# Moving the second pair's preparation, dropping idle matmuls and copies' engine in early attention, and moving stores to GpSimd with sums loaded ahead in a fused attention and two-MLP kernel

## The chip, the cores and the metric

One Trainium2 chip, one of its cores. The metric is device time in microseconds (us) of one execution; the kernel before was run three times, and its median counts. TensorE is PE in the profile (its weight loads are PEld), VectorE is DVE, ScalarE is ACT, GpSimd is POOL, SyncE is SP. SPq and POOLq are the queues on which SP and POOL issue transfers (DMAs).

## The reference

Attention over 4 batches, 8 heads, 576 positions and 64 columns a head, with a causal mask and a bias from running sums of `s`; its output, 2304 tokens of 512 columns, goes through two MLPs (512 to 2048 to 512) with different activations:

```python
scores = scale * np.matmul(q, k.transpose(0, 1, 3, 2))
cum = np.cumsum(np.maximum(s, 0.0), axis=-1)
bias = -(cum[:, :, :, None] - cum[:, :, None, :])
scores = np.where(causal, -1000000000.0, scores + np.minimum(bias, 0.0))
attn = np.exp(scores - np.max(scores, axis=-1, keepdims=True))
attn = attn / (np.sum(attn, axis=-1, keepdims=True) + 1e-09)
x = np.matmul(attn, v)                       # heads side by side: 2304 x 512
h = x @ w_in1;  x = (h / (1 + np.exp(-1.702 * h))) @ w_out1
h = x @ w_in2;  P = a[0] + a[1]*h + a[2]*h*h + a[3]*h*h*h
Q = 1 + abs(b[0]) * abs(h) + abs(b[1]) * h*h
return (P / (Q + 1e-6)) @ w_out2
```

## The kernel before, in words

**Numbers.** Every fp32 operand of a product is split into a high and a low part, and a product is three matmuls (high by high, and the two mixed ones). Weights are split on the chip: `convert` loads half a unit of weights (512 KB, tile `raw`, in attention `stgA`) on SP's queue (L493, L495), works on it with ACT (L497, L499, L505) and DVE (L500, L501, L502, L504, L506; in attention L504 and L506 are POOL's), and leaves high and low parts in `u` or, for units that have no room yet, in `park`. `park` then writes these two parts to scratch memory `wd` (L542), and `fetch` reads a whole unit back later (L546). `raw` has four buffers.

**Attention** is one loop over j, 80 units (4 batches, 4 pairs of heads, 5 blocks of rows in the order 0, 1, 4, 2, 3; five units make a pair, twenty a batch). For unit j TensorE makes the scores (L251), DVE adds the mask and finds the row minimum (L285), ACT takes the exponential (L292), POOL scales the rows (L304). Three units later (two from j = 20) the rows are transposed on TensorE (L344; L323 and L327 for block 4) and copied out of PSUM by ACT, or by DVE where `COPY_V` names the (batch, block) (L351, L348, L324, L328); another unit later come the products with the values (L370). The operands of a pair are made one pair ahead by `prep`, a generator in two steps: transposes of k and then of q (L218), high parts on ACT (L176), low parts on DVE (L179), and copies of parts to other partitions by transfers on SP's queue (`kh<-kh` and `k<-qs`, L225). It also loads the bias rows (`k<-rows`, L204) that `store_sums` wrote before (L115 on SP, L113 on POOL). `pair_load` loads k and q of a pair (L145) and, when its `values` is called, v (L152, L156).

Between the steps of a unit `fill` puts work of the first MLP's units 0 to 4 for the batch before (`mlp1_first`: stage1 L562, out1 L586), paid by a credit of `FILL` / 20 a unit. While there is none yet (`cold`, up to j = 22) it issues `warm` instead: matmuls on zeros whose result nobody reads (L75). In attention the order on TensorE is that of the code; elsewhere, and on the other engines, a scheduler sets it.

**Behind attention** `mlp1_rest` runs the first MLP's units 5 to 11, and then 12 to 15, over 8 blocks of 288 tokens. A step (blk, j) is stage1 of one unit, its activation (`act1`: ACT L573, DVE L574, ACT L576, DVE L579) and, two steps later, out1 into four PSUM banks `a`. With the last unit of a block, four sums of earlier passes are loaded (`xp`, L636, SP), DVE adds them (L637), and the result is stored (L638, SP). `tick` issues half a conversion a step: units 12 to 15 first, then units 7 to 15 of the second MLP by way of `park`. Then comes the second MLP (`mlp2`: L562, L727).

SP issues its transfers in one order; one that waits holds up those behind it.

Of the kernel before, what the change touches and what calls it, by code (L numbers as in the profile page):

```python
# [10 lines left out]
F32 = mybir.dt.float32  # L11
# [5 lines left out]
ALU = mybir.AluOpType  # L17
# [12 lines left out]
P = 128  # L30
NQ = 5
KD = DM // P
NF = DF // P
F1 = 5
HB = S // 2
# [9 lines left out]
FILL = 33.0  # L45
AHEAD, AHEAD_0 = 2, 3
COPY_V = ((0, 0), (0, 4))
# [8 lines left out]
class Fused:  # L56
# [340 lines left out]
    def attention(self, att, mlp):  # L397
# [7 lines left out]
        nprep = iter(())  # L405
        self.sums_load(att)
        ld = self.pair_load(att, 0, 0, True)
# [4 lines left out]
        ld = self.pair_load(att, 0, 1)  # L412
        start()
        ld["values"]()
        self.store_sums()
        done = 0
        for j in range(n + AHEAD + 1):
# [16 lines left out]
            q = FILL / 20  # L434
            if j < n:
                self.unit_scores(att, units[j], 0)
                if j:
                    next(nprep, None)
            self.fill(q / 3, 1)
# [8 lines left out]
            if j < n and idx == 4:  # L448
                for _ in nprep:
                    pass  # L450
                g = b * NP + p + 2
                if g < NB * NP:
                    ld = self.pair_load(att, *divmod(g, NP))
                    ld["values"]()
            if k >= 0:
                self.unit_values(att, units[k])
# [78 lines left out]
    def park(self, buf, layer, f, half):  # L535
        nc = self.nc
        key = layer, f
        if half == 0:
            self.parked[key] = self.dram.tile([P, 4, 512], F32, name=f"wd{layer}_{f}")
        self.convert(self.source(layer, f, half), buf[:, 0], buf[:, 1])  # L540
        for i in range(2):
            nc.sync.dma_start(self.parked[key][:, half + 2 * i], buf[:, i].bitcast(F32))  # L542
# [79 lines left out]
    def mlp1_rest(self, pool, fs, src, dst, after_unit, at_block, last):  # L622
        nc = self.nc
        nblk = 2 * NB
        pend = []

        def flush():
# [3 lines left out]
            if j == len(fs) - 1:  # L631
                for d in range(KD):
                    st = self.spool.tile([P, HB], F32, name="st", tag="st", bufs=2)
                    xp = self.spool.tile([P, HB], F32, name="xp", tag="xp", bufs=2)
                    sl = np.s_[d * P : (d + 1) * P, blk * HB : (blk + 1) * HB]
                    nc.sync.dma_start(xp, src[sl])  # L636
                    nc.vector.tensor_tensor(st, accs[d][:, :HB], xp, ALU.add)  # L637
                    nc.sync.dma_start(dst[sl], st)  # L638
# [3 lines left out]
        for blk in range(nblk):  # L642
# [6 lines left out]
            for j, f in enumerate(fs):  # L649
# [12 lines left out]
                pend.append((blk, j, f, g, accs))  # L662
                self.tick()
# [247 lines left out]
```

## Time and profile before

| what | value |
|---|---|
| median of 3 runs (lowest, highest) | 1064.91 us (1062.80, 1066.14) |
| the profiled execution: time, span | 1062.4 us, 1060.6 us |
| busy in it: PE, PEld | 1029.6 us (97%), 942.3 us (89%) |
| busy in it: DVE, ACT, POOL | 805.7 us (76%), 722.8 us (68%), 259.4 us (24%) |
| chain that ended last, by engine | PE 73%, DMA 12%, DVE 6%, ACT 5% |

Attention ends near 327 us, the first MLP near 666 us. A busy PE is not a PE at its peak: the ends of matmuls are modelled, so how many matmuls of one shape fit into a stretch says more than the busy share. The share of the span is an average over stages with different limits; what a change in one stage is worth is read from the rows of that stage.

### The profile page before, as it was taken

Reading aid. Unit: us, or ns where it says so; the run is one execution under the profiler, and the core shown is the slowest. Engines: PE = TensorE matmul, PEld = TensorE weight load, DVE = VectorE, ACT = ScalarE, POOL = GpSimd, SP = SyncE. Lnnn points to the kernel's source line nnn. Section 1 sums busy time; section 2 is a strip of 40 time slices with the busy share of each in tenths; the row PEclk is TensorE's granted clock in tenths of the full one; section 3 lists DMA queues with packets and bytes.
Section 4 is the critical chain, followed back from the end, with each engine's and each line's share of the span. In section 5 each row is a group of like instructions: output and inputs, shape, how many; then the busy total and the mean of one; then the engine's idle time right before and its main releaser. Section 6 shows DMA issues by size and latency. Waiting matters only on the chain.

```text
span 1060.6 us, 19849 instructions
## 1 busy us (share of the span) xinstructions
PE 1029.6 (97%) x7073; PEld 942.3 (89%) x7073; DVE 805.7 (76%) x1874; ACT 722.8 (68%) x1668; POOL 259.4 (24%) x321
## 2 busy tenths in 40 slices
PE   6998999999999999998999999999999999999997
PEld 4767998898999899988999999998999999999996
DVE  6787767766644998884379344898998988989886
ACT  6898868978855675563265224787777777777765
POOL 4455734543420000000000000222222222222222
PEclk8999999999999999999999999999999999999999
DMA  8456455543215648995146546100010010100000
GB/s 183 120 153 163 112 148 157 137 138 82 53 46 222 204 160 277 300 305 175 46 125 209 188 124 243 48 30 30 2 47 14 15 46 1 31 30 1 31 1 30
DMA packets 88203, 117.31 MB, mean 111 GB/s; under 512 B 25728, under 2 KB 71808, under 8 KB 86508
## 3 DMA queue, kind: packets, MB, share of 16 engines
q1 hardware_dynamic: 87688, 115.43, 36.3%
q8 instruction: 56, 0.92, 0.4%
q0 software_dynamic: 192, 0.31, 0.2%
q14 instruction: 43, 0.35, 0.1%
q10 hardware_dynamic: 224, 0.30, 0.1%
HBM read 75.08 MB, written 32.05 MB: 101 GB/s over the span
## 4 chain that ended last, share of the span: by engine, by line
PE 73%; DMA 12%; DVE 6%; ACT 5%; issue 2%; POOL 1%; SPq 0%; ACTq 0%; DVEq 0%; POOLq 0%
PE h L562 29%; PE a L727 18%; PE a L586 12%; DMA raw<-in_moe_w_out_dram 5%; PE s L251 5%; PE O L370 4%; PE tp L344 2%; DMA stgA<-in_moe_w_in_dram 2%; DMA raw<-in_moe_w_in_dram 2%; DMA xp<-x 1%; DVE cvx L504 1%; DMA wd<-park 1%; ACT cvx L499 1%; DVE gl L579 1%; DVE cvx L502 1%
## 5 line engine op out<-in xcount | busy, mean ns | idle before, releaser
L710 POOL TENSOR_TENSOR gl<-u,gh 128x384 fp32r<-128x384 f32 x96 | 105.5, 1099 | 625.9 <-DMA x<-st 339.3
L562 PE MATMUL h<-x,u 128*128 128x288 f32 x1536 | 234.5, 298 | 5.3 <-ACT st L600 1.6
L586 PE MATMUL a<-gh,u 128*128 128x288 f32 x1024 | 232.3, 299 | 4.1 <-DVE st L637 3.0
L562 PEld LDWEIGHTS h<-x,u 128*128 128x128 f32 x1536 | 212.8, 188 | 11.2 <-DVE g L574 3.1
L586 PEld LDWEIGHTS a<-gh,u 128*128 128x128 f32 x1024 | 172.4, 188 | 10.2 <-DVE st L637 2.8
L562 PE MATMUL h<-y,u 128*128 128x384 f32 x864 | 166.2, 336 | 0.0
L562 PEld LDWEIGHTS h<-y,u 128*128 128x128 f32 x864 | 153.0, 188 | 6.3
L586 PE MATMUL a<-gl,u 128*128 128x288 f32 x512 | 148.6, 296 | 1.2 <-DVE gl L579 1.2
L727 PE MATMUL a<-u,gh 128*128 128x512 f32 x432 | 114.9, 394 | 0.9 <-ACT gh L708 0.9
L304 POOL TENSOR_SCALAR bt<-bt,sm 128x128 f32<-128x128 f32 (+3 forms) x129 | 71.3, 563 | 113.8 <-DVE sm L301 59.7
L586 PEld LDWEIGHTS a<-gl,u 128*128 128x128 f32 x512 | 96.3, 188 | 2.6 <-DVE gl L579 1.8
L292 ACT ACTIVATE bt<-bt,mn 128x128 f32<-128x128 f32 (+3 forms) x129 | 74.8, 580 | 29.7 <-DVE mn L285 28.1
L727 PEld LDWEIGHTS a<-u,gh 128*128 128x128 f32 x432 | 80.0, 188 | 14.9 <-ACT gh L708 1.7
L285 DVE CUSTOM_DVE_ANT_0 bt<-s,mask 128x128 f32<-128x128 f32 (+3 forms) x129 | 62.3, 483 | 37.1 <-PE s L251 31.2
L573 ACT ACTIVATE g<-h 128x288 f32<-128x288 f32 x128 | 51.1, 405 | 56.8 <-PE h L562 51.9
L576 ACT ACTIVATE gh<-g 128x288 fp32r<-128x288 f32 x128 | 55.7, 442 | 48.0 <-DVE g L574 47.3
L708 ACT ACTIVATE gh<-u 128x384 fp32r<-128x384 f32 x96 | 50.6, 527 | 54.2 <-DVE u L706 53.2
L693 ACT ACTIVATE y<-h,cf 128x384 f32<-128x384 f32 x96 | 55.6, 579 | 38.6 <-PE h L562 38.6
L574 DVE SCALAR_TENSOR_TENSOR g<-g,h 128x288 f32<-128x288 f32 x128 | 56.9, 448 | 32.4 <-ACT g L573 32.1
L251 PE MATMUL s<-k 68*128 68x256 f32 (+2 forms) x192 | 72.5, 382 | 8.7 <-DVE qs L179 4.8
L698 DVE SCALAR_TENSOR_TENSOR y<-s,cf,y 128x384 f32<-128x384 f32 x96 | 59.4, 618 | 24.5 <-ACT s L695 23.5
L706 DVE SCALAR_TENSOR_TENSOR u<-y,u 128x384 f32<-128x384 f32 x96 | 72.7, 757 | 1.1
(115 smaller groups left out, 2014.5 us busy)
## 6 DMA issues: line engine op xcount, KB each, us to landing
raw<-in_moe_w_in_dram SPq DMA_DIRECT2D x24, 512.0 KB
raw<-in_moe_w_out_dram SPq DMA_DIRECT2D x24, 512.0 KB
x<-st SPq DMA_DIRECT2D x64, 144.0 KB
wd<-park SPq DMA_DIRECT2D x36, 256.0 KB
u<-wd SPq DMA_DIRECT2D x8, 1024.0 KB
x2p<-st SPq DMA_DIRECT2D x32, 144.0 KB
xp<-x2p SPq DMA_DIRECT2D x32, 144.0 KB
xp<-x SPq DMA_DIRECT2D x32, 144.0 KB
```

The lines of the kernel that those rows point to most:

```text
L251: nc.tensor.matmul(sc[: c1 - c0, :w], lhsT=q[:, c0:c1], rhs=k[:, j0 : j0 + w], start=m == 0, stop=m == 1,)
L285: nc.vector.tensor_tensor_reduce(bt[:, j0 : j0 + w], sc[:, :w], mask, 1.0, 3.0e38 if i == 0 else mn[:, 0:1], ALU.add, ALU.min, mn[:, i : i ...
L292: ex = nc.scalar.activation(bt[:, :n], bt[:, :n], AF.Exp, bias=mn[:, i : i + 1], scale=-1.0, accum_out=sm[:, col : col + 1],)
L304: nc.gpsimd.tensor_scalar(bt[:, :n], bt[:, :n], inv[:, i : i + 1], 1.0, ALU.mult, ALU.mult)
L562: nc.tensor.matmul(ps_tile, lhsT=u[:, wl, kk * P : (kk + 1) * P], rhs=x(xl, kk), start=(n == 0), stop=(n == 3 * KD - 1),)
L574: nc.vector.scalar_tensor_tensor(g[:, :w], g[:, :w], 1.0, h, ALU.add, ALU.mult)
L576: nc.scalar.activation(gh[:, :w], g[:, :w], AF.Copy)
L586: nc.tensor.matmul(acc, lhsT=u[:, wl, d * P : (d + 1) * P], rhs=g[gl], start=(first and i == 0), stop=(last and i == 2),)
L698: nc.vector.scalar_tensor_tensor(y, s, cf[:, 7:8], y, ALU.mult, ALU.add)
L706: last = nc.vector.scalar_tensor_tensor(p, y, 2.0, p, ALU.subtract, ALU.mult)
L710: nc.gpsimd.tensor_tensor(gl, p, gh.bitcast(F32), ALU.subtract)
L727: nc.tensor.matmul(accs[m], lhsT=g[gl][:, m * P : (m + 1) * P], rhs=u[:, wl, :], start=(f == 0 and i == 0), stop=(f == NF - 1 and i == 2),)
```

## The change

In attention: `prep` of the second pair starts in unit 0 instead of unit 1; the stores of the sums are issued ahead of the first two pairs' values, and the second pair's values in unit 2; from j = 4 a cold unit issues its matmul on zeros only where j is a multiple of 5 (15 fewer); the filler's credit is 30 instead of 33 up to j = 42; DVE instead of ACT copies blocks 0, 1 and 4 of the second batch. Behind attention: the stores of parked parts and of the sums are issued on POOL; the four sums of a block are loaded in its third step, and the addition writes into the loaded tile, so that one set of four tiles takes the place of two tiles `st` and two `xp`.

```diff
--- before.py
+++ after.py
@@ -42,9 +42,9 @@
 PACE = 0.5
 AHEAD_F = (5, 6, 7)
 AHEAD_J = (35, 39, 43, 47, 51, 55)
-FILL = 33.0
+FILL, FILL_1 = 33.0, 30.0
 AHEAD, AHEAD_0 = 2, 3
-COPY_V = ((0, 0), (0, 4))
+COPY_V = ((0, 0), (0, 4), (1, 0), (1, 1), (1, 4))
 W2_SLOTS = 7
 CONV_J = (9, 12, 15, 18, 20, 22, 24, 26, 28, 30)
 CONV = [(f, 0) for f in range(F1)] + [(f, 1) for f in range(F1)]
@@ -410,9 +410,8 @@
             pass
         start = ld["values"]
         ld = self.pair_load(att, 0, 1)
+        self.store_sums()
         start()
-        ld["values"]()
-        self.store_sums()
         done = 0
         for j in range(n + AHEAD + 1):
             i = max(j - (AHEAD_0 if j < 20 else AHEAD), -1)
@@ -431,12 +430,11 @@
             if i >= 0 and i < n and units[i][0] and i % 20 == 1:
                 self.filler = chain(self.filler, self.mlp1_first(mlp, units[i][0] - 1))
                 self.cold = False
-            q = FILL / 20
+            q = (FILL_1 if j < 43 else FILL) / 20
             if j < n:
                 self.unit_scores(att, units[j], 0)
-                if j:
-                    next(nprep, None)
-            self.fill(q / 3, 1)
+                next(nprep, None)
+            self.fill(q / 3, j < 4 or j % 5 == 0)
             if 0 <= i < n:
                 tr = self.unit_transpose(att, units[i])
                 next(tr, None)
@@ -452,6 +450,8 @@
                 if g < NB * NP:
                     ld = self.pair_load(att, *divmod(g, NP))
                     ld["values"]()
+            if j == 2:
+                ld["values"]()
             if k >= 0:
                 self.unit_values(att, units[k])
             self.fill(q / 3, j < 4)
@@ -538,8 +538,9 @@
         if half == 0:
             self.parked[key] = self.dram.tile([P, 4, 512], F32, name=f"wd{layer}_{f}")
         self.convert(self.source(layer, f, half), buf[:, 0], buf[:, 1])
+        eng = nc.gpsimd if self.wide else nc.sync
         for i in range(2):
-            nc.sync.dma_start(self.parked[key][:, half + 2 * i], buf[:, i].bitcast(F32))
+            eng.dma_start(self.parked[key][:, half + 2 * i], buf[:, i].bitcast(F32))
 
     def fetch(self, u, layer, f):
         self.units[layer, f] = u
@@ -623,6 +624,18 @@
         nc = self.nc
         nblk = 2 * NB
         pend = []
+        xps = {}
+
+        def area(blk, d):
+            return np.s_[d * P : (d + 1) * P, blk * HB : (blk + 1) * HB]
+
+
+        def sums(blk):
+            xps[blk] = []
+            for d in range(KD):
+                xp = self.spool.tile([P, HB], F32, name="xp", tag="xp", bufs=KD)
+                nc.sync.dma_start(xp, src[area(blk, d)])
+                xps[blk].append(xp)
 
         def flush():
             blk, j, f, g, accs = pend.pop(0)
@@ -630,12 +643,9 @@
                 self.out1(accs[d][:, :HB], self.units[1, f], d, g, j == 0, j == len(fs) - 1)
             if j == len(fs) - 1:
                 for d in range(KD):
-                    st = self.spool.tile([P, HB], F32, name="st", tag="st", bufs=2)
-                    xp = self.spool.tile([P, HB], F32, name="xp", tag="xp", bufs=2)
-                    sl = np.s_[d * P : (d + 1) * P, blk * HB : (blk + 1) * HB]
-                    nc.sync.dma_start(xp, src[sl])
-                    nc.vector.tensor_tensor(st, accs[d][:, :HB], xp, ALU.add)
-                    nc.sync.dma_start(dst[sl], st)
+                    xp = xps[blk][d]
+                    nc.vector.tensor_tensor(xp, accs[d][:, :HB], xp, ALU.add)
+                    nc.gpsimd.dma_start(dst[area(blk, d)], xp)
             if blk == nblk - 1:
                 after_unit(f)
 
@@ -660,6 +670,8 @@
                 if accs is None:
                     accs = [self.bank("a", f"a2_{blk}_{f}_{d}") for d in range(KD)]
                 pend.append((blk, j, f, g, accs))
+                if j == 2:
+                    sums(blk)
                 self.tick()
         while pend:
             flush()
```

SP's order at the start, in the program before. `kn`, `qn` and `vn` are k, q and v of a pair, numbered by pair; `kh_1` and `k_1` belong to the second pair:

```order
L115 DMA rows<-stgA 16x2x576 x4
L145 DMA kn_2_369<-in_k_dram 96x2x384
L145 DMA qn_2_371<-in_q_dram 96x2x384
L204 DMA k_1_244<-rows 4x2304
L493 DMA stgA<-in_moe_w_in_dram 128x4x256
L81 DMA cf<-in_moe_a_dram 128x4
L82 DMA cf<-in_moe_b_dram 128x2
L145 DMA kn_3_596<-in_k_dram 96x2x384
L145 DMA qn_3_598<-in_q_dram 96x2x384
L225 DMA kh_1_242<-kh_1_242 64x1152
L225 DMA k_1_244<-qs_1_243 64x1152
```

And after the change, the four stores `rows<-stgA` standing just ahead of these rows:

```order
L152 DMA vn_1_193<-in_v_dram 128x4x64
L156 DMA vn_1_193<-in_v_dram 64x2x64
L204 DMA k_1_219<-rows 4x2304
L145 DMA kn_2_368<-in_k_dram 96x2x384
L145 DMA qn_2_370<-in_q_dram 96x2x384
L145 DMA kn_3_591<-in_k_dram 96x2x384
L493 DMA stgA<-in_moe_w_in_dram 128x4x256
L225 DMA kh_1_217<-kh_1_217 64x1152
L145 DMA qn_3_593<-in_q_dram 96x2x384
L81 DMA cf<-in_moe_a_dram 128x4
L82 DMA cf<-in_moe_b_dram 128x2
L225 DMA k_1_219<-qs_1_218 64x1152
```

The loads of k and q of the third pair moved from ahead of the bias rows of the second pair to behind them, and `k_1<-qs_1` stands behind the same loads as before.

SP's order behind attention, where unit 9 of the second MLP is parked, before:

```order
L493 DMA raw<-in_moe_w_in_dram 128x4x256
L542 DMA wd_9_6428<-park 128x512
L495 DMA raw<-in_moe_w_out_dram 128x1024
L542 DMA wd_9_6428<-park 128x512
L638 DMA x_12_5460<-st 128x288
L636 DMA xp<-x2p 128x288
L638 DMA x_12_5460<-st 128x288
L636 DMA xp<-x2p 128x288
L542 DMA wd_9_6428<-park 128x512
L493 DMA raw<-in_moe_w_in_dram 128x4x256
```

And after, at the same conversions:

```order
L493 DMA raw<-in_moe_w_in_dram 128x4x256
L495 DMA raw<-in_moe_w_out_dram 128x1024
L493 DMA raw<-in_moe_w_in_dram 128x4x256
L495 DMA raw<-in_moe_w_out_dram 128x1024
L493 DMA raw<-in_moe_w_in_dram 128x4x256
L637 DMA xp<-x2p 128x288
L495 DMA raw<-in_moe_w_out_dram 128x1024
L637 DMA xp<-x2p 128x288 x3
L493 DMA raw<-in_moe_w_in_dram 128x4x256
L495 DMA raw<-in_moe_w_out_dram 128x1024
```

No store is left between the loads of raw weights, only loads of sums.

POOL's order behind its last scaling of rows in attention; before, the next instruction there was the second MLP's first L710, and these rows now stand in between:

```order
+L648 DMA x_12_5445<-xp 128x288 x4
+L543 DMA wd_7_6071<-park 128x512 x4
+L543 DMA wd_8_6234<-park 128x512 x3
+L648 DMA x_12_5445<-xp 128x288 x4
+L543 DMA wd_8_6234<-park 128x512
+L543 DMA wd_9_6409<-park 128x512 x4
+L543 DMA wd_10_6564<-park 128x512 x4
+L543 DMA wd_11_6739<-park 128x512 x4
+L648 DMA x_12_5445<-xp 128x288
+L543 DMA wd_12_6898<-park 128x512
```

The stores of sums (L648) and of parked parts (L543) moved to POOL in the order in which they become ready.

## Rows read from the trace of the kernel before

**Rows 1.** Stretches: microseconds, busy time and instructions by engine, granted clock, DMA share, GB/s.

```profile
400.00:500.00 100.00, 94.10 (x679) 90.46 (x679) 79.29 (x175) 55.38 (x120) 0.00 (x0) 1.00 0.85 273
500.00:600.00 100.00, 100.00 (x757) 100.00 (x757) 62.88 (x141) 42.85 (x93) 0.00 (x0) 1.00 0.39 124
```

**Rows 2.** Whom PE waited for, 400 to 500 us: total, times, longest.

```profile
PE a L586 <- DVE st L637: 3.0, 3, 1.4
PE h L562 <- DVE g L574: 1.5, 4, 0.5
```

**Rows 3.** Groups of ACT, 400 to 500 us: busy, mean ns, idle time before, releasers.

```profile
L497 ACT ACTIVATE raw<-raw 128x512 int32<-128x512 uint32 x23 | 15.7, 681 | 34.5 <-DMA raw<-in_moe_w_in_dram 17.2 <-DMA raw<-in_moe_w_out_dram 17.1
```

**Rows 4.** Whom SP's queue waited for, 400 to 500 us.

```profile
SPq L542 <- ACT gh L576: 19.3, 9, 4.6
SPq L542 <- DVE park L506: 6.2, 10, 1.2
```

**Rows 5.** SP's queue in order of time, from 443 us: start, us, what.

```profile
443.34 0.32 SPq L542 DMA_DIRECT2D wd<-park  x1
443.75 0.87 SPq L638 DMA_DIRECT2D x<-st  x2
...
445.71 0.38 SPq L495 DMA_DIRECT2D raw<-in_moe_w_out_dram  x1
```

**Rows 6.** ACT in order of time; in brackets the idle time before and its releaser.

```profile
451.10 0.67 ACT L497 ACTIVATE raw<-raw 128x512 int32<-128x512 uint32 x1 [3.80 <-DMA raw<-in_moe_w_out_dram]
```

**Rows 7.** DVE in order of time.

```profile
437.81 0.68 DVE L504 CUSTOM_DVE_ANT_0 cvx<-raw,cvx 128x1024 uint16<-128x1024 uint16 x1
...
494.93 0.46 DVE L637 TENSOR_TENSOR st<-a,xp 128x288 f32<-128x288 f32 x1 [2.27 <-DMA xp<-x2p]
```

**Rows 8.** SP's queue in order of time, 10 to 22 us.

```profile
10.63 0.47 SPq L152 DMA_DIRECT2D vn<-in_v_dram  x1
...
11.87 1.99 SPq L115 DMA_DIRECT2D rows<-stgA  x4
13.96 0.36 SPq L145 DMA_DIRECT2D kn<-in_k_dram  x1
...
15.74 0.26 SPq L204 DMA_DIRECT2D k<-rows  x1
...
21.07 0.49 SPq L225 DMA_DIRECT2D k<-qs  x1
```

**Rows 9.** The chain that ended last, 20 to 28 us: start, us, what.

```profile
21.07 5.89 DMA k<-qs
```

**Rows 10.** PE in order of time, from 27 us.

```profile
27.09 0.35 PE L251 MATMUL s<-k 68*128 68x256 f32 x1 [3.29 <-DMA k<-qs]
...
31.98 0.38 PE L75 MATMUL idle<-mask 128*128 128x512 bf16 x1
32.20 0.49 PE L344 MATMUL tp<-ident,bt 128*128 128x128 f32 x3
```

**Rows 11.** Stretches of early attention, columns as in the first group.

```profile
27.90:31.30 3.40, 3.40 (x20) 2.51 (x18) 2.24 (x11) 2.65 (x8) 1.15 (x2) 0.50 0.32 92
31.30:41.00 9.70, 9.70 (x97) 7.77 (x97) 7.74 (x30) 7.80 (x23) 3.75 (x7) 1.00 0.41 96
41.00:86.00 45.00, 41.66 (x384) 31.55 (x382) 37.59 (x137) 40.29 (x111) 24.66 (x34) 1.00 0.66 173
86.00:110.00 24.00, 20.38 (x157) 17.17 (x158) 17.46 (x55) 20.50 (x56) 15.72 (x19) 0.93 0.49 128
```

**Rows 12.** Groups of DVE: L500 at 30 to 320 us, then at 330 to 500 us.

```profile
L500 DVE TENSOR_SCALAR stgA<-stgA 128x512 f32<-128x512 f32 x16 | 8.5, 533 | 6.5 <-ACT stgA L499 6.4
L500 DVE TENSOR_SCALAR cvx<-cvx 128x512 f32<-128x512 f32 x38 | 15.9, 422 | 10.5 <-ACT cvx L499 10.5
```

**Rows 13.** Groups of POOL, up to 330 us: its stores of rows.

```profile
L113 POOL DMA_DIRECT2D rows<-stgA x4 | 2.0, 503 | 0.0
```

**Rows 14.** Groups of DVE, 30 to 320 us: a copy of block 4.

```profile
L324 DVE COPY pt<-tp 128x512 f32<-128x512 f32 x4 | 2.7, 686 | 0.8 <-PE tp L323 0.6
```

## The prediction

> **What bounds the kernel now.** I read the busy line first: PE 97%. That alone says nothing about where time can be won, so I cut the span into stretches and counted matmuls instead of busy time. From 500 us to the end of the first MLP, and all through the second, TensorE runs without gaps: 757 matmuls of 288 columns in 100 us, 132 ns each [rows 1]. From 400 to 500 us, with the same kind of matmul, there are 679, 78 fewer, or 78 x 0.132 = 10.3 us lost; by busy time it is 5.9 us, since ends are modelled. So behind attention there is up to 10.3 us to win in this stretch, and next to nothing after it. In early attention the losses are of another kind: one wait of 3.29 us for a transfer at 27 us [rows 10], then a stretch at the lower of the two clocks [rows 11], and from 41 us on ACT busy 40.29 of 45 us, with DVE at 37.59 [rows 11]. Later attention, with filler, keeps PE busy.
>
> Then who is waited for in 400 to 500 us. PE names DVE: additions L637, 3.0 us, and activations L574, 1.5 us [rows 2]. But DVE is not the cause: it is busy 79 of 100 us [rows 1]. Ahead of it ACT stands idle 34.5 us in front of L497, waiting for raw weights to land [rows 3], and ACT works in order, so the activation that PE needs stands behind L497. And the loads are late because SP's queue is: it spends 19.3 and 6.2 us in front of stores of parked parts that are not computed yet [rows 4]. One case shows the size. The load issued at 445.71 [rows 5] writes the raw buffer that DVE's L504 at 437.81 was last to read, so it could have gone at 438.5; SP issued it 7.2 us later, behind a parked store at 443.34 and two stores of sums. ACT then waited 3.80 us for it [rows 6]. A second, smaller cause: DVE itself waited 2.27 us for a sum at 494.93 [rows 7], which is asked for only when it is needed.
>
> **The change, part by part.**
>
> *Stores on POOL, sums ahead.* Removed from SP: 36 parked stores (9 units, 2 halves, 2 parts) and 64 stores of sums (2 passes, 8 blocks, 4 each); POOL has no instruction in that stretch [rows 1], so it can wait in their place, and only later stores are queued behind one that waits. Each load of raw weights then waits for its buffer alone, about 7 us sooner in the case above, which is more than the longest wait of ACT there, 3.80 us. I expect ACT's 34.5 us in front of L497 to fall below 10, and the loads of sums, now asked for some five steps ahead in a block of seven, not to be waited for by DVE. A new wait is added: a load of sums needs the store of the block before to have landed, since they share a tile, and raw loads stand behind it on SP; it is issued a step after that store, and the block is long. What does not go away: DVE is still at 79%, the DMA engines at 0.85 [rows 1], with the same bytes to move. Bounds: nothing, and 10.3 us. I take 7.0, two thirds, nearer the upper end, because the cause is queueing in SP and not a full engine.
>
> *Second pair sooner.* PE waits until 27.09 us for `k<-qs` of the second pair, issued at 21.07 and landed 5.89 us later [rows 8 to 10]. The change lets ACT finish its high parts sooner, and with them the issue. But the transfer itself is the long part: it stands behind the same loads as before, and these now start later. Before, k of the third pair was issued at 13.96, ahead of the bias rows, which had to wait until 15.74. After, it stands behind the bias rows. Their wait moves from 15.74 to about 14.5, because the stores of sums go where the loads of values went (from 11.87 to 10.63 [rows 8]); so k goes at about 14.8 instead of 13.96. The queue of transfers starts 0.8 us later and holds as much, so `k<-qs` lands no sooner. Bounds: a gain of 3.3 us, the whole wait; a loss of 0.8. I take a loss of 0.5.
>
> *Fewer zeros.* A matmul on zeros takes TensorE 0.22 us (from 31.98 to 32.20, [rows 10]); 15 go, 3.3 us in all. Where PE sets the pace, 31.3 to 41 us (9.70 of 9.70 [rows 11]), four go: 0.9 us. The other ones lie mostly under ACT. Bounds 0 and 3.3; I take 1.0.
>
> *Copies on DVE, even filler.* 16 copies change engine; one of block 4 takes DVE 686 ns [rows 14]. ACT is the busier at 86 to 110 us (20.50 of 24, DVE 17.46 [rows 11]); afterwards PE is full and hides both. The filler's work is the same in all and only spread over two units more. Bounds: four copies of 0.69 us lost where DVE is late just then, 2.8; the same gained where ACT is. I take 0.
>
> Sum: -7.0 + 0.5 - 1.0 = -7.5 us. On the profiled execution's 1062.4 that is 1054.9; the median of the runs lies 2.5 us above that execution, so 1057 is what I give.
>
> **A rule against the change.** L500, which works on one input in SBUF, takes DVE 422 ns where POOL has nothing to do and 533 on average beside POOL's work in attention [rows 12]; so the two engines do get in each other's way. From 400 to 500 us 23 conversions begin [rows 3], 46 such instructions with L501, and some 50 stores will now be issued on POOL beside them, at 0.50 us of POOL each by the nearest, smaller stores [rows 13]. At +0.11 us each that is 5.1 us of DVE, against 21 us that it stands idle [rows 1]: nothing on the path, and the sum stays -7.5. At the far end, each of the 46 held up for a whole store, 23 us, DVE's room is used up and the 7.0 with it. I take the first, since DVE's stretched average was measured beside POOL work of many lengths. The Trainium skill, SBUF — State Buffer, "Who interferes with whom", speaks for the second: GpSimd writes the descriptors of a DMA that it issues through a port pair shared with VectorE, whoever comes first holds it for a whole two-port instruction, and the page advises the other queues. The trace agrees that an overlap costs; no run here shows it for such a store.
>
> **The rivals.**
> - *The wait moves to the engines that carry the loads.* The DMA share is already 0.85; if loads land late because the engines are full, issuing them sooner changes little. For it: 0.85 is the mean of the whole 100 us. Against it: that mean holds although SP stood 25.5 of them in front of parked stores [rows 4]. Then only the waits for sums go, of which 2.27 us is the longest [rows 7], and 0.5 more for zeros less the later pair: 1065 - 2.8 = 1062.
> - *POOL and DVE hold each other up (slower).* The place is the 46 instructions L500 and L501 of the rule above; it decides from 21 / 46 = 0.46 us each, where DVE's idle time is used up. If they stretch by 0.6, just over one store, DVE needs 27.6 us more, 6.6 over its room, and the old 10.3 stay lost: 1065 + 6.6, less 0.5 for zeros and the later pair: 1071.
> - *The second pair does come sooner.* If transfers overlap better than in order, the 3.3 us go, and the stretch at half clock behind them too, 3.40 us at 0.50 [rows 11], 1.7 us: 1057 - 5 = 1052.
> - *Too few zeros.* Granted clock fell to 0.50 (1.2 of 2.4 GHz) after TensorE had stood idle for 3.29 us [rows 10, 11], and a stretch of 3.40 us then does half its work, 1.7 us lost. With 15 fillers gone, other thin places might fall too; three falls cost 5.1 and leave 1062. The Trainium skill, TensorE: Matmul & The Clock Gate, "What's actually happening", says that the slow clock is the default and that activity releases it, which speaks against removing idle matmuls; by the rows, units after 31 us have PE at 9.70 of 9.70, zeros being a small part.
>
> **How the numbers follow.** Chances: forecast 0.48; second pair sooner as well 0.15; DMA engines full 0.20; POOL against DVE 0.10; clock 0.07. The forecast's own range is 1053 to 1061. For 8 in 10 I take in the sooner pair and the full engines, and leave out the slow rival and the far ends: 1049 to 1066. A measurement of this kernel can tell about 0.3%, 3.2 us, from no change. Faster: 0.48 + 0.15, and a fifth of the 0.27 of the two cases at 1062, 0.05: 0.68. Same: most of the rest of those, 0.19. Slower: 0.13, the POOL rival's 0.10 and the far end of those two, 0.03.
>
> **What would show it.** Right: 400 to 500 us holds over 730 matmuls; ACT's idle time before L497 is under 10 us; no wait of DVE on `xp`; SP's queue waits for buffers alone; PE still waits some 3 us for `k<-qs` near 27 us. Wrong: L500 and L501 well above 422 ns behind attention; new stretches at 0.50 between 41 and 110 us; loads of sums that wait for POOL's stores with raw loads behind them; a parked store so late that DVE's L506 waits for its buffer.

## The result, and the profile after

The changed kernel takes 1068.86 us (median of six runs, 1067.31 to 1071.61) where the kernel before took 1064.74 beside it: a ratio of 1.0052, with a 95% interval of 1.0034 to 1.0070. It is slower, by about 5 us, and outside the range of 1049 to 1066. The profiled execution took 1069.57 us with a span of 1067.8.

Where the time went shows in one row of each trace: VectorE's last addition behind attention (L381), first the kernel before, then the changed one. The numbers at the end of the first part are the start of the first and the last such instruction.

```profile
L381 DVE TENSOR_TENSOR x<-O,x x48: 210/417/425, 36.1 to 328.0; 128x256 fp32r<-128x256 f32 x32, 128x64 fp32r<-128x64 f32 x16
```

```profile
L381 DVE TENSOR_TENSOR x<-O,x x48: 209/417/425, 37.4 to 335.9; 128x256 fp32r<-128x256 f32 x32, 128x64 fp32r<-128x64 f32 x16
```

Attention ends at 335.9 in the place of 328.0 us, 7.9 us later. The same view of the first matmul of the second MLP (`a<-u,gh`) has 672.9 in the place of 666.0, 6.9 us later. So 7.9 us are lost up to the end of attention, and only 1.0 comes back behind it, where I had forecast 7.

Stretches of the changed kernel (columns as in [rows 1]; the granted clock is the third number from the end):

```profile
27.80:41.50 13.70, 13.01 (x80) 10.72 (x78) 7.17 (x27) 7.57 (x23) 3.01 (x6) 0.50 0.36 87
41.50:51.70 10.20, 8.59 (x81) 6.64 (x80) 8.40 (x32) 8.56 (x25) 3.42 (x5) 1.00 0.36 92
51.70:58.50 6.80, 6.80 (x49) 5.80 (x46) 4.53 (x16) 4.83 (x13) 4.15 (x6) 0.50 0.65 163
58.50:85.80 27.30, 23.95 (x222) 18.33 (x222) 22.49 (x80) 22.40 (x62) 13.57 (x18) 1.00 0.57 147
85.80:89.30 3.50, 3.50 (x23) 2.79 (x21) 2.77 (x9) 3.45 (x13) 2.01 (x3) 0.51 0.64 164
400.00:500.00 100.00, 93.67 (x682) 91.81 (x681) 84.94 (x190) 58.79 (x123) 29.17 (x52) 0.98 0.84 275
500.00:600.00 100.00, 100.00 (x757) 100.00 (x756) 62.16 (x143) 43.77 (x95) 13.71 (x25) 1.00 0.40 129
```

Before, TensorE's clock stood at 0.50 for 3.40 us behind its wait at 27 us and was back at 1.00 by 31.30 [rows 11]; now it stays at 0.50 (1.2 of 2.4 GHz) for 13.70 us, falls again at 51.70 for 6.80 and at 85.80 for 3.4. PE reads 13.01 of 13.70 us busy in the first of these stretches: the busy line does not show that the matmuls run slower, the number of matmuls does (80, where [rows 11] have 97 in 9.70 us at full clock). Behind attention there are 682 matmuls from 400 to 500 us, against 679 before and the 730 that I had named as a sign.

The wait at 27 us itself is hardly changed. PE of the changed kernel in order of time:

```profile
23.05 0.44 PE L370 MATMUL O<-pt,vn 128*64 128x128 f32 x4
26.40 0.35 PE L251 MATMUL s<-k 68*128 68x256 f32 x1 [2.92 <-DMA k<-qs]
```

Behind attention, whom SP's queue waited for from 400 to 500 us, and then ACT's group L497 in the same stretch:

```profile
SPq L493 <- DVE cvx L504: 33.3, 9, 6.2
SPq L637 <- DMA x<-xp: 25.5, 7, 7.2
SPq L495 <- DVE cvx L504: 20.3, 10, 4.2
```

```profile
L497 ACT ACTIVATE raw<-raw 128x512 int32<-128x512 uint32 x23 | 15.7, 682 | 30.2 <-DMA raw<-in_moe_w_in_dram 15.5 <-DMA raw<-in_moe_w_out_dram 14.7
```

The waits for parked stores [rows 4] are gone from SP. In their place stand 25.5 us in which the loads of sums (L637) wait for the stores of the block before, and ACT's idle time in front of L497 is 30.2 us where it was 34.5 [rows 3], not below 10. One instance has the longest stall there. SP's queue, then ACT, then PE, in order of time:

```profile
421.45 0.33 SPq L495 DMA_DIRECT2D raw<-in_moe_w_out_dram  x1
428.78 0.33 SPq L637 DMA_DIRECT2D xp<-x2p  x1
429.27 0.38 SPq L493 DMA_DIRECT2D raw<-in_moe_w_in_dram  x1
```

```profile
434.76 0.65 ACT L497 ACTIVATE raw<-raw 128x512 int32<-128x512 uint32 x1 [5.71 <-DMA raw<-in_moe_w_in_dram]
435.32 0.64 ACT L499 ACTIVATE cvx<-raw 128x512 f32<-128x512 f32 x1
435.86 0.43 ACT L577 ACTIVATE gh<-g 128x288 fp32r<-128x288 f32 x1
```

```profile
432.87 0.30 PE L587 MATMUL a<-gh,u 128*128 128x288 f32 x1
436.34 0.80 PE L587 MATMUL a<-gh,u 128*128 128x288 f32 x4 [3.17 <-ACT gh L577]
```

SP issues nothing between 421.8 and 428.78, a raw load goes out behind a load of sums, ACT waits 5.71 us for it, and the `gh` that PE needs stands behind L497 in ACT's order. That looked like what limits the whole stretch; an experiment (small_park) corrected it.

### The profile page after: what moved, and what is told of

It reads as the page before. It is cut to its first block, busy times and chain, and to the rows that moved or that the text cites. A ratio compares the mean times of both kernels' runs of the same rounds, so it can differ in the third digit from the quotient of the medians.

```text
span 1067.8 us, 19863 instructions
## 1 busy us (share of the span) xinstructions
PE 1033.3 (97%) x7058; PEld 950.1 (89%) x7058; DVE 813.2 (76%) x1890; ACT 718.8 (67%) x1652; POOL 315.2 (30%) x421
## 4 chain that ended last, share of the span: by engine, by line
PE 76%; DMA 8%; ACT 5%; DVE 5%; issue 4%; POOL 2%; SPq 0%; ACTq 0%; POOLq 0%; DVEq 0%
PE h L563 30%; PE a L739 18%; PE a L587 14%; PE s L251 5%; PE O L370 4%; PE tp L344 3%; DMA raw<-in_moe_w_out_dram 3%; DMA raw<-in_moe_w_in_dram 2%; DMA stgA<-in_moe_w_in_dram 1%; POOL wd L543 1%; ACT cvx L499 1%; DMA k<-qs 1%; ACT bt L292 1%; PE tk L218 1%; PE tq L218 1%
## 5 line engine op out<-in xcount | busy, mean ns | idle before, releaser
L563 PE MATMUL h<-x,u 128*128 128x288 f32 x1536 | 232.1, 298 | 4.4 <-DVE g L575 2.6
L648 POOL DMA_DIRECT2D x<-xp x64 | 35.3, 552 | 224.4 <-DVE g L575 94.9
L292 ACT ACTIVATE bt<-bt,mn 128x128 f32<-128x128 f32 (+3 forms) x129 | 74.8, 580 | 34.0 <-DVE mn L285 31.3
L251 PE MATMUL s<-k 68*128 68x256 f32 (+2 forms) x192 | 74.8, 393 | 8.5 <-DMA k<-stgA 4.6
L710 DVE SCALAR_TENSOR_TENSOR y<-s,cf,y 128x384 f32<-128x384 f32 x96 | 59.3, 618 | 20.7 <-ACT s L707 19.5
```

The costliest lines, as they stand in the source:

```text
L251: nc.tensor.matmul(sc[: c1 - c0, :w], lhsT=q[:, c0:c1], rhs=k[:, j0 : j0 + w], start=m == 0, stop=m == 1,)
L292: ex = nc.scalar.activation(bt[:, :n], bt[:, :n], AF.Exp, bias=mn[:, i : i + 1], scale=-1.0, accum_out=sm[:, col : col + 1],)
L563: nc.tensor.matmul(ps_tile, lhsT=u[:, wl, kk * P : (kk + 1) * P], rhs=x(xl, kk), start=(n == 0), stop=(n == 3 * KD - 1),)
L710: nc.vector.scalar_tensor_tensor(y, s, cf[:, 7:8], y, ALU.mult, ALU.add)
```

## The experiments

All times are against the kernel before on the same chip. I held two theories from this reading. First: attention lost its 7.9 us to TensorE's clock, and the new order, the copies and the missing zeros matter only through it; the rival is that loads or copies come late by themselves. Second: behind attention the loads of sums hold raw loads up on SP's queue; the rival is that the engines that carry the transfers set the pace.

The table gathers the results. "Clock" is the mean granted clock of the profiled execution from 20 to 137 us, "attention" the start of its last L381, "MLP 2" the start of the first matmul of the second MLP.

| Kernel | ratio to before | 95% interval | clock | attention | MLP 2 |
|---|---|---|---|---|---|
| before | 1 | | 0.97 | 328.0 | 666.0 |
| changed | 1.0052 | 1.0034–1.0070 | 0.88 | 335.9 | 672.9 |
| front_only | 1.0059 | 1.0039–1.0080 | 0.96 | 332.6 | 670.1 |
| behind_only | 0.9974 | 0.9956–0.9993 | 1.00 | 324.7 | 660.9 |
| zeros_back | 1.0011 | 0.9994–1.0028 | 0.97 | 329.8 | 665.5 |
| zeros_only | 1.0024 | 1.0006–1.0042 | 0.96 | 329.1 | 669.0 |
| order_only | 1.0047 | 1.0030–1.0063 | 0.96 | 330.1 | 671.5 |
| copies_only | 1.0046 | 1.0028–1.0064 | 0.93 | 334.1 | 674.8 |
| zeros_in_wait | 0.9993 | 0.9977–1.0010 | 0.97 | 328.5 | 663.3 |
| before_zeros_in_wait | 0.9948 | 0.9928–0.9968 | 1.00 | 326.2 | 664.3 |
| order_zeros_in_wait | 0.9971 | 0.9956–0.9986 | 1.00 | 326.2 | 665.2 |
| copies_zeros_in_wait | 0.9992 | 0.9977–1.0007 | 1.00 | 327.4 | 664.1 |
| zeros_back_and_in_wait | 0.9965 | 0.9946–0.9984 | 0.99 | 327.2 | 662.1 |
| behind_zeros_in_wait | 0.9962 | 0.9946–0.9977 | 0.97 | 327.9 | 662.4 |
| behind_more_zeros | 1.0004 | 0.9986–1.0022 | 0.97 | 331.2 | 666.6 |
| best_of_parts | 0.9954 | 0.9934–0.9973 | 0.99 | 327.0 | 664.0 |
| sums_later | 1.0039 | 1.0021–1.0057 | 0.91 | 334.9 | 673.0 |
| parks_only | 0.9978 | 0.9965–0.9991 | 0.97 | 328.1 | 664.3 |
| sums_pool | 1.0112 | 1.0092–1.0133 | 0.99 | 326.3 | 664.3 |
| small_park | 0.9922 | 0.9906–0.9939 | 0.97 | 327.4 | 657.7 |

**The change in halves.** front_only takes `attention`, FILL_1 and COPY_V from the changed kernel and the rest from before; behind_only the reverse (`park` and `mlp1_rest`); zeros_back has

```diff
-            self.fill(q / 3, j < 4 or j % 5 == 0)
+            self.fill(q / 3, 1)
```

in the changed kernel.

> The attention part of the change alone (order, zeros, copies on VectorE, even filler); behind attention as before. Theory: the loss sits here. In the trace of the changed kernel the end of attention is 7.8 us later than before, and behind attention 0.9 us comes back; of the 4.1 us between the medians this part should then cost about 5: 1070 us, with the granted clock at 0.50 over more than 3.4 us behind 27 us. Rival: attention's lateness belongs to that one execution, and the loss is made behind attention: 1065 us, no change.

> The part behind attention alone (stores of parked parts and sums on GpSimd's queue, sums loaded ahead); attention as before. Theory: it brings next to nothing, since the loads of sums wait on SP's queue for the stores of sums of the block before (46.4 us of waits from 403 to 518 us in the changed kernel) and hold raw loads up in the place of the stores that are gone: 1064 us, within 2 of before. Rival: the part does bring what I predicted and the changed kernel loses it elsewhere: 1058 us.

> The changed kernel with one matmul on zeros ahead of each unit of the first batch again, 15 more; all else as changed. Theory: without them TensorE's granted clock stays at 0.50 for 13.7 us behind 27.8 us and falls again at 51.7 for 6.8 us; with them it comes back after 3.4 us as before and does not fall at 51.7: extra 17 us at half clock are 8.5 us of work, of which some was hidden, so 5 us less than the changed kernel, 1064 us. Rival: the order of loads and copies makes attention late, and the clock is a result: 1068 to 1069 us, with the stretches at 0.50 as in the changed kernel.

front_only costs 0.59% (6.3 us), behind_only brings 0.26% (2.8 us): the loss sits in attention. behind_only lies between the two theories for it (1064 and 1058): 1060.5. With the zeros back the changed kernel loses most of its loss, 1.0011, as the first theory says; but not all, since without any attention part it would be at 0.9974. Two of the slow stretches of the changed kernel, in zeros_back:

```profile
27.80:41.50 13.70, 13.41 (x111) 10.94 (x112) 9.04 (x37) 9.17 (x26) 3.22 (x7) 0.75 0.36 88
51.70:58.50 6.80, 6.73 (x61) 4.91 (x59) 4.61 (x18) 4.71 (x13) 2.96 (x5) 1.00 0.68 176
```

The first holds 111 matmuls at a clock of 0.75, where the changed kernel has 80 at 0.50; the second 61 at full clock, where it has 49.

**The parts of attention alone.** zeros_only is the reverse of the line above, in the kernel before. order_only is

```diff
         start()
-        ld["values"]()
-        self.store_sums()
...
-                if j:
-                    next(nprep, None)
+                next(nprep, None)
...
+            if j == 2:
+                ld["values"]()
             if k >= 0:
```

with `self.store_sums()` ahead of `start()`. copies_only has FILL_1 and the longer COPY_V alone.

> The kernel before with the 15 matmuls on zeros left out, and nothing else of the change. Theory: they alone hold TensorE's granted clock up in the first batch; with the zeros back the changed kernel came to 1.0011 of before where it was 1.0052, so leaving them out costs 4.3 us: 1068 us, with stretches at 0.50 between 27 and 110 us beyond the 6.8 us of before. Rival: the zeros matter only where the new order has already thinned TensorE's work; on the old order they cost nothing: 1064 us.

> The kernel before with the new order of the second pair alone (sums stored first, first pair's values next, second pair's at j of 2, its preparation one half unit sooner). Zeros and copies as before. With the zeros back the changed kernel is at 1.0011 and the part behind attention alone at 0.9974, so order and copies together cost some 3.9 us. Theory: the order is what costs, 1067 us, since loads of later pairs stand behind others. Rival: the copies on VectorE cost it, the order nothing or a gain up to 3.3 us: 1060 to 1064 us.

> The kernel before with the copies of blocks 0, 1 and 4 of the second chunk on VectorE and the evener filler alone. Order alone cost 0.47%, zeros alone 0.24%, all three 0.59%. Theory: by these the copies give 0.12% back, 1062.4 us, since ACT is the busier from 86 to 110 us. Rival: they cost nothing and bring nothing, 1063.6, and the three parts share losses.

Leaving zeros out costs 0.24% alone, the order 0.47%, the copies 0.46%, where I had expected a small gain of the copies: a miss. All three together cost 0.59%, so the parts do not add up; they seem to share a loss. In order_only the second pair comes no sooner (PE waits 3.46 us for `k<-qs`, until 27.51), and the clock behind it stays low for longer:

```profile
27.00:37.30 10.30, 9.57 (x58) 8.02 (x60) 5.27 (x21) 4.95 (x15) 2.08 (x4) 0.50 0.27 72
37.30:137.00 99.70, 92.64 (x821) 75.76 (x826) 80.14 (x272) 87.08 (x240) 60.42 (x77) 1.00 0.56 143
```

This longer fall does not hold the whole loss: of the 5.5 us by which order_only's second MLP starts later than before's, 2.1 stand at the end of attention, and the other 3.4 come behind it, where the edit changes nothing.

**Is it the clock?** These kernels put 12 matmuls on zeros into TensorE's wait, ahead of the first scores of the second pair:

```diff
+            if j == 5:
+                self.warm(12)
             if j < n:
                 self.unit_scores(att, units[j], 0)
```

zeros_in_wait is the changed kernel with them, order_zeros_in_wait, copies_zeros_in_wait, behind_zeros_in_wait and before_zeros_in_wait are the kernels of those names with them.

> The changed kernel with 12 matmuls on zeros (2.6 us at 0.22) put where TensorE stands idle 2.92 us for the second pair's k, and nothing else. Theory: the idle time there is what brings the clock to 0.50 from 27.8 us on, and the thin units behind it keep it there for 13.7 us; with zeros in the wait the stretch goes, and half of 13.7 us at half clock, 5 to 7 us, comes back: 1063 us. Rival: the new order makes the units behind the wait late by themselves (loads, ACT), and the clock is only seen there: 1068 us, and stretches at 0.50 between 27 and 60 us stay above 10 us.

> The new order alone, with the 12 matmuls on zeros in the wait of TensorE for the second pair's k. Theory: what the order costs alone (0.47%, profile with 10.3 us at 0.50 behind the wait against 3.4 before) is the clock behind that wait; with zeros there it comes to the kernel before or below: 1062 us. Rival: the order delays loads that later units need: 1067 us, with the half clock gone and the time not.

> The copies and the evener filler alone, with the 12 matmuls on zeros in the wait. Copies alone were at 1.0046, against what I expected. Theory: that too is the clock behind the wait (6.8 us at 0.50 there, and 10.2 more until 136 us): 1062 to 1064 us. Rival: copies on VectorE and the filler's other placing cost by themselves behind 100 us: 1067 us, with the lateness at 35 us gone and that behind 100 us left.

> The whole change with all zeros of before, and the 12 in the wait beside them. Zeros back alone gave 1.0011, zeros in the wait alone 0.9993, the part behind attention alone with zeros in the wait 0.9962. Theory: the two kinds of zeros do one thing, hold the clock, and with both the attention part costs nothing: 1060 us (0.9965). Rival: order or copies cost something that no zero gives back: 1063 us.

> The kernel before with the 12 matmuls on zeros in the wait alone, the base of the runs that have them. Theory: it loses 3.4 us at 0.50 behind the wait in most executions and 3.4 near 103 us; the zeros give back 1 to 2 us of that: 1062 us (0.9985). Then the new order with the zeros, 0.9971, is a gain of its own of some 1.5 us, as a sooner second pair would be. Rival: the zeros alone bring the whole of it: 0.9971.

PE of zeros_in_wait in order of time: of the 2.92 us of idle time 0.52 are left.

```profile
23.44 0.44 PE L370 MATMUL O<-pt,vn 128*64 128x128 f32 x4
23.81 2.76 PE L75 MATMUL idle<-mask 128*128 128x512 bf16 x12
27.09 0.35 PE L251 MATMUL s<-k 68*128 68x256 f32 x1 [0.52 <-DMA k<-qs]
```

The second pair's k lands no sooner in this kernel (TensorE goes on at 27.09 us, in the changed kernel at 26.40), and still it goes from 1.0052 to 0.9993: 12 matmuls whose output nobody reads bring 6 us. The order alone goes from 1.0047 to 0.9971. The whole change with both kinds of zeros is at 0.9965, level with behind_zeros_in_wait (0.9962): with them the attention part costs nothing. And the kernel before gains as well, more than I had expected, 0.9948: with the 3.29 us of [rows 10] filled, its clock reads 1.00 from 20 to 137 us:

```profile
20.00:137.00 117.00, 109.42 (x951) 87.71 (x950) 93.19 (x318) 100.07 (x275) 66.57 (x88) 1.00 0.54 141
```

Since before gains too, these runs must be compared with before_zeros_in_wait. Against it the order costs 0.23%, where it cost 0.47% without zeros in the wait; what is left is not clear of noise.

Each execution, not only the profiled one, has its mean granted clock on record. 0.001 of it over the span is 1.06 us of TensorE's work at full clock, so a difference in it gives an estimate of the most that the clock by itself can have cost. The changed kernel's six runs have 0.981 to 0.988 (mean 0.9843), with the zeros back the mean is 0.9905, and all runs of before lie at 0.988 to 0.997. The means of single parts, each with before beside it:

| Kernel | clock | before | worth, us | measured, us |
|---|---|---|---|---|
| front_only | 0.9890 | 0.9938 | 5.1 | 6.3 |
| zeros_only | 0.9898 | 0.9924 | 2.8 | 2.6 |
| order_only | 0.9912 | 0.9924 | 1.3 | 5.0 |
| copies_only | 0.9908 | 0.9937 | 3.1 | 4.9 |
| before_zeros_in_wait | 0.9950 | 0.9930 | -2.1 | -5.5 |

The clock is enough for what the missing zeros cost, and for most of the attention part as a whole. It is not enough for the order alone, the copies alone, or the whole gain from filling the wait of the kernel before.

One rival is untested. Zeros are not all that these edits move: on the other engines the scheduler sets the order, and it changes with them. ACT behind the wait, first in the changed kernel, then in zeros_in_wait:

```profile
27.23 0.72 ACT L176 ACTIVATE kh<-tk 64x288 fp32r<-64x288 f32 x2 [2.09 <-PE tk L218]
27.84 0.39 ACT L292 ACTIVATE stgA<-stgA,mn 128x128 f32<-128x128 f32 x1
```

```profile
27.92 0.43 ACT L176 ACTIVATE kh<-tk 64x288 fp32r<-64x288 f32 x1 [2.36 <-PE tk L218]
28.24 0.38 ACT L292 ACTIVATE stgA<-stgA,mn 128x128 f32<-128x128 f32 x1
28.53 0.19 ACT L292 ACTIVATION_READ_ACCUMULATOR stgA<-stgA,mn 128x1 f32 x1
28.62 0.87 ACT L176 ACTIVATE kh<-tk 64x288 fp32r<-64x288 f32 x2
```

An exponential (L292) now stands ahead of the second high part of k (L176), not behind it. In zeros_only and zeros_back the order differs on ACT, DVE and POOL over much of early attention, and for some loads on SP. No run holds that order fixed, so how much of the gain is its doing stays open.

Copies_zeros_in_wait moved by as much as the others, to 0.9992, but stays 0.44% behind before_zeros_in_wait, as copies_only stays 0.46% behind before. Its profile has the clock at 1.00 and attention only 1.2 us later than that of before_zeros_in_wait. Yet zeros_back_and_in_wait has these copies too and is level with the kernel without them. What the copies cost beyond the clock is not settled.

**Adding up.**

> The part behind attention alone, with the same 12 matmuls on zeros in the wait. Theory: before and this kernel fall to 0.50 for about 3.4 us behind the wait in most executions, 1.7 us: 1059 us against 1060.5 without the zeros. Rival: the fall there costs nothing by the end, since ACT and DVE set the pace from 41 us on: 1060.5.

> The part behind attention alone with the 12 zeros in the wait and two zeros in the place of one ahead of each unit of the first batch. Theory: the clock then falls nowhere between 20 and 130 us (6.8 us at 0.50 in the profile with one), 3.4 us; 15 more zeros cost 3.3 us where TensorE sets the pace, less elsewhere: 1058 to 1060 us, no clear gain over one zero, 1059.3. Rival: more zeros delay the units themselves: 1062 us.

> The part behind attention, the new order, and the 12 zeros in the wait; zeros, copies and filler as before. Theory: gains add up, 0.9974 behind attention and 0.9971 for order with zeros: 1058 us (0.9945). Rival: both sat in the same 3 to 4 us of clock: 1060 us (0.9962), as the part behind attention with zeros alone.

behind_more_zeros is behind_zeros_in_wait with `self.fill(q / 3, 2)`. More zeros ahead of every unit cost 0.42% against one: attention ends at 331.2. No sum of parts is clearly better than before_zeros_in_wait alone; best_of_parts (0.9954) and behind_zeros_in_wait (0.9962) lie within its interval. All three beat both kernels.

**Behind attention.** sums_later asks for the sums at `j == min(4, len(fs) - 1)` in the place of `j == 2`; sums_pool has `nc.gpsimd.dma_start(xp, ...)` in behind_only; parks_only is before with the `eng` of `park` alone; small_park is behind_only with

```diff
-            eng.dma_start(self.parked[key][:, half + 2 * i], buf[:, i].bitcast(F32))
+            eng.dma_start(self.parked[key][:, half + 2 * i, :(512 if key[0] == 1 or key[1] == 7 else 32)], buf[:, i, :(512 if key[0] == 1 or key[1] == 7 else 32)].bitcast(F32))
...
-        self.nc.sync.dma_start(u.bitcast(F32), self.parked[layer, f])
+        self.nc.sync.dma_start(u.bitcast(F32), self.parked[layer, f if layer == 1 else 7])
```

so that of the units 8 to 15 of layer 2 only a sliver is stored and unit 7 is read in their place.

> The changed kernel with the four loads of sums asked for at step 4 of a block (at its last step in the pass of four) in the place of step 2, so that the stores they wait for have landed. Theory: SP's queue then waits for raw buffers alone, the stall of 3.34 us at 436 us and the half clock behind it (3.4 us) go: 4 to 5 us less than the changed kernel, 1064 us. Rival: the DMA engines, busy 0.86 there, set the pace of the raw loads: SP's waits for sums go, ACT's idle time in front of L497 stays near 31 us, and the time stays 1068 to 1069 us.

> The part behind attention alone, with the loads of sums on GpSimd's queue too, so that on SP's queue raw loads wait for their buffers alone (in the changed kernel moving the request two steps later left the loads of sums at the same places of the queue, so that run told nothing). Theory: the loads of sums hold raw loads up; without that the longest stall of TensorE there (3.3 us, and 3.4 us at half clock behind it) goes: 1056 us, against 1060.5 with them on SP. Rival: the DMA engines set the pace, ACT's waits in front of L497 stay near 31 us: 1060 us. Third way: parked stores stand behind loads of sums that wait on GpSimd, and conversions wait for the parked buffers: 1063 us.

> The kernel before with the parked stores on GpSimd's queue, sums loaded and stored on SP's as before. Theory: the DMA engines set the pace of the raw loads, so SP's free queue brings little: 1062 to 1063 us, and the rest of the 3 us of the part behind attention came from the sums loaded ahead (TensorE waited 3.0 us for the additions L637). Rival: the parked stores are the whole gain: 1060.5 us.

> The part behind attention alone, but of eight of its nine parked units only 32 of 512 columns are stored, and the first unit is read back in the place of all (part of the weights is wrong by that); waits and their order stay, some 7.9 MB of 27 in 100 us go. Theory: loads of sums on SP's queue hold the raw loads up, whatever the engines carry: ACT's idle time in front of L497 stays above 25 us (31.1 with all stored) and the time within 2 us of 1060.5. Rival: the DMA engines, at 0.85, set the pace: idle time below 15 us, and 1055 us.

sums_later tells nothing of its question: the scheduler, which orders each queue by its own estimates, put the loads of sums at the same places of SP's queue, so it is the changed kernel timed a second time (1.0039). In sums_pool SP waited for buffers alone, as intended, but from 326.3 to 664.3 it takes 338.0 us as before does (328.0 to 666.0), and behind_only takes 336.2: no gain. Its 1.12% lie in the second MLP, whose ACT work the scheduler had ordered anew (8.4 us of PE's waits for `gh` from 513 us on, 0.9 in the kernel before), so its total says nothing of the queue. parks_only brings most of behind_only's gain, 0.22 of 0.26%.

small_park decides between queue and engines. Stretch 400 to 500 us, first of behind_only, then of small_park; then PE's waits, SP's waits and ACT's group in small_park:

```profile
400.00:500.00 100.00, 95.36 (x701) 94.14 (x700) 78.53 (x175) 56.81 (x120) 29.20 (x52) 0.98 0.84 272
400.00:500.00 100.00, 98.84 (x739) 97.80 (x738) 81.55 (x181) 58.43 (x126) 30.08 (x52) 1.00 0.63 199
```

```profile
PE a L587 <- DVE gl L580: 0.9, 1, 0.9
PE h L563 <- DVE g L575: 0.2, 1, 0.2
```

```profile
SPq L637 <- DMA x<-xp: 38.0, 9, 15.3
```

```profile
L497 ACT ACTIVATE raw<-raw 128x512 int32<-128x512 uint32 x24 | 16.4, 681 | 30.6 <-DMA raw<-in_moe_w_in_dram 17.7 <-DMA raw<-in_moe_w_out_dram 12.9
```

SP waits for sums as long as in behind_only (39.1 us there), longer than in the changed kernel, and still TensorE does 739 matmuls where behind_only has 701 and the changed kernel 682; the time falls by another 0.52%. So with these waits in place the traffic (DMA share 0.63 in the place of 0.84) sets the pace, and the second theory falls. The rival's own sign failed too: ACT's idle time in front of L497 did not fall, 30.6 us (29.1 in behind_only). Most of it is idle time that ACT has to spare. The longest of these waits did shrink, 5.7 us in the changed kernel, 5.3 in behind_only, 3.9 here, and PE's own waits with them; that this is the way by which the bytes reach PE is argued, not shown.

## Why the prediction was wrong, point by point

*Fewer zeros* (-1.0): the step that failed. I priced 15 matmuls by the time that they take, 0.22 us each, and gave the clock a chance of 0.07 at 5.1 us. Alone the edit costs 0.24%, 2.6 us; in the whole change its return brought 0.41%, 4.4 us. The place and the mechanism were in the rival, "new stretches at 0.50 between 41 and 110 us" among the signs; I set its chance by PE's busy time after 31 us (9.70 of 9.70), and busy time does not tell whether the clock holds: the changed kernel's stretch at 0.50 has PE at 13.01 of 13.70. The Trainium skill, TensorE: Matmul & The Clock Gate, "What's actually happening", has the slow clock as the default and activity as what releases it. The trace agrees where the wait is filled (1.00 from 20 to 137 us in before_zeros_in_wait); that thin but nearly unbroken work would stay at 0.50, I had not read out of it.

*Second pair sooner* (+0.5): right as to the wait, wrong as to the price. `k<-qs` was issued 1.7 us sooner (19.39, before 21.07 [rows 8]), took 6.87 us where it took 5.89 [rows 9], so it landed 0.7 us sooner, and PE's wait is 2.92 us. But the edit cost 0.47% alone. Part of that is the clock behind the wait, at 0.50 for 10.3 us where it was 3.40; with zeros in the wait the order costs 0.23% against before_zeros_in_wait. The rest stays open.

*Copies and even filler* (0, bounds ±2.8): 0.46% alone, outside my bounds. Its profile has the clock at 0.93 from 20 to 137 us, but two of the falls (6.80 us from 27.2 and 3.40 from 51.1) lie ahead of its first changed instruction, a copy on VectorE at 85.25 us, so they are not the edit's. What the edit costs by itself stays open.

*Stores on POOL, sums ahead* (-7.0, bounds 0 to -10.3): right in sign, too large; 0.26%, 2.8 us. The mis-sized step was "because the cause is queueing in SP and not a full engine". The rival with the full engines had 2.3 us for this part (its 2.8 are for the whole change), close to the 2.8 measured. In that it was partly lucky: it drew the gain from the waits for sums alone, and parks_only, which leaves these as they were, has 0.22 of the 0.26%. The new wait that I named came (25.5 us for sums on SP) but was not what held the gain down.

*POOL and DVE hold each other up*: did not happen. L500 from 330 to 500 us, where POOL now has work (52 instructions from 400 to 500 us), takes 423 ns on average, without it 422 [rows 12]. In the second line the three numbers are the shortest, the median and the longest:

```profile
L500 DVE TENSOR_SCALAR cvx<-cvx 128x512 f32<-128x512 f32 x38 | 16.1, 423 | 17.7 <-ACT cvx L499 17.6
L500 DVE TENSOR_SCALAR cvx<-cvx x38: 412/422/467, 349.3 to 492.4; 128x512 f32<-128x512 f32 x38
```

The rule of the Trainium skill against the change (SBUF — State Buffer, "Who interferes with whom") is thus not borne out for this instruction and these stores: the longest of the 38 took 467 ns, 45 more than the average without, where the far end had 0.50 us more for each.

The sum with what was measured: +6.3 for attention and -2.8 behind it are +3.5; the changed kernel is at +5.5 by its ratio, with about 1.9 to either side. Both halves were off in the same direction.

## What to carry to other kernels

A matmul on zeros beside a stalled TensorE is not only a cost of 0.22 us but can be a hold on the clock: before such work is taken out, or work before a wait is moved, read the granted clock stretch by stretch, and count matmuls, not busy time. Where TensorE must wait some 3 us for a transfer, try filling that wait with matmuls on zeros of about its length: that alone brought 0.52% here, more than any part of the change. More is not better: a second one ahead of every unit cost 0.42%. Where the transfer engines are as full as here (a share of 0.84), moving stores to another queue brought little (0.26%), fewer bytes more (another 0.52%).

## What the runs showed of the hardware that I had not expected

The clock's falls differ from execution to execution of the same instructions. Before, behind_only, parks_only, sums_pool and small_park run attention by the same instructions in the same order on every engine; their profiles have the mean clock from 20 to 137 us at 0.97, 1.00, 0.97, 0.99 and 0.97, and attention ends at 328.0, 324.7, 328.1, 326.3 and 327.4. The changed kernel, sums_later and front_only share another attention in the same way: 0.88, 0.91 and 0.96, and it ends at 335.9, 334.9 and 332.6. So 3.4 us between two profiles can be the draw alone, and one profile is not enough for an edit of this size; whether the runs of one kernel draw independently of each other no run here shows, and the smaller ratios are to be read with that in mind. Over all rows of the table, attention tends to end the later the lower that clock (324.7 to 327.4 us at 1.00, 334.1 to 335.9 at 0.93 and below), but not strictly: at 0.96 it ends between 329.1 and 332.6. front_only has almost the clock of before (0.96 and 0.97) and its attention still ends 4.6 us later, so a part of the loss does not show in this clock; where that part comes from stays open.
